# Conversion steps behind each slot's product, the states' last rows written in place, and x2 loads issued by GpSimd

## The chip, the cores and the metric

The kernel runs on one core of one Trainium2 chip. The metric is the device time of one execution in microseconds (us), as the median of three runs.

## What is computed

Attention between tokens and states in both directions, then two feed-forward layers over all 4608 rows (8 blocks of 512 token rows and 32 state rows):

```python
scores = scale * np.matmul(x, state.transpose(0, 1, 3, 2))   # x: (8, 8, 512, 64), state: (8, 8, 32, 64)
a = softmax(scores)                                          # with 1e-9 added to the sum
xread = np.matmul(a, state)
a2 = softmax(scale * np.matmul(state, x.transpose(0, 1, 3, 2)))
sread = np.matmul(a2, x)
x = concat([xread, sread]) -> (4352, 512)
h = ((x @ w1) * (x @ w2)) @ w3                               # w1, w2: 512 x 1024, w3: 1024 x 1024
x2 = h @ w_out                                               # 1024 x 512
h = x2 @ w_in                                                # 512 x 2048
out = (h * np.clip(h + 3.0, 0.0, 6.0) / 6.0) @ w_out2        # 2048 x 512
```

All inputs are float32.

## The kernel before

Matmuls take float32 operands split in a high part, rounded by ScalarE (`rnd`, L71), and the rest, made by VectorE (`rest`, L79); `mm3` (L87 to L90) multiplies the three products that matter. The order of the instructions on every engine is the order in which the program issues them.

The first part, up to about 480 us, goes over eight blocks `b` of the batch. The weights w3 and w_out are multiplied together ahead of it, and state and w1, w2 are folded into products p (`p_mm`, `p_split`), so that a block is eight **slots** `m`. A slot (`slot`, L646) does on TensorE two groups of six matmuls into the PSUM banks ps_ab, and ScalarE copies the first (asb, L522) while VectorE multiplies the second with it (ab, L524). Then `before()` runs, in which the next block's attention takes a step. Then x2_one multiplies an ab of two slots earlier with w3p; half-way through, `mid` splits this slot's ab (abh on ScalarE, abl on VectorE), and in slots of even number multiplies and splits the p that the slots from m + 2 on use (ph on ScalarE, pl on VectorE); attention takes another step there. Over a block attention's steps are scores in slot 0 (two banks ps_s), exponentials in slot 2, two transposes in slot 4 (ps_e) and the state read in slot 6 (ps_r); each is followed by the x2_one matmuls of the second half.

ps_ab, ps_p, ps_s, ps_e and ps_r take four PSUM banks in turn (`bank`, bufs=4). So the tile four allocations back must have been read out before a bank is written again.

Beside this runs the conversion of the second layer's weights (`stream2`, L426): 16 units, each in steps on VectorE (ts, hd, w, sl, cm), ScalarE (hd from raw, sh) and SP (the load raw, and writes of sh and sl to DRAM). A step counts 2 to 4 units of work, and ROOM says how many a slot may take; after `slot` returned, the loop took that many steps (L770 to L772):

```python
                slot(b, m, A, before, mid_)
                if b == 0:
                    step()
                room += ROOM[m]
                while room > 0:
                    room -= next(second, 99)
```

The load of the next x (`load_x`, L175: br and xr) is issued on SP in slot 6, in block 0 in slot 7.

In block 6 nothing is left to convert; w1 and w2 are split there for the states (`ws_split`, L570), five of eight, with five buffers. At the start of block 7 `s_block` (L577) passes all 256 state rows through the layer, eight steps of 24 matmuls of 256 columns (ps_sb). The state rows, sread's output, went to DRAM block by block (xs to xsd, L235) and come back in one load (xs_r, L744). The last three splits were made ahead of step 4, when their buffers were free.

The second part handles pairs `p` of blocks: `gates` (L927's matmuls, two levels of sums that save one of eight products), then `output` in 28 steps `v` of 12 matmuls (L1088). Step v splits the operand hlj of step v + 2 in a ring of three, high half on ScalarE and low half on VectorE, and `side(v)` takes steps of `combos(p + 1)`, which loads the next pair's x2 in two halves k (`x2_load`, L599: two DMAs each into the only buffer r), makes sums and splits them (xc). `per` tells how many combos steps a v takes. SP also issues all weight loads (`w_load`, L809), each of which waits until TensorE has let a buffer go. GpSimd issues the DMAs that add one g to another (`t_sum`, L895).

Of the kernel before, what the change touches and what calls it, by code (L numbers as in the profile page):

```python
# [7 lines left out]
F32 = mybir.dt.float32  # L8
F32R = mybir.dt.float32r
# [10 lines left out]
def attn_moe_kernel(tc, xt_d, xn_d, bd_d, wa, wb, wc, wi, wo, out):  # L20
# [48 lines left out]
    def rnd(out_, in_, eng):  # L69
        if eng == "A":  # L70
            nc.scalar.activation(out=out_, in_=in_, func=AF.Copy)  # L71
        elif eng == "P":
            nc.gpsimd.tensor_scalar(out=out_, in0=in_, scalar1=1.0, scalar2=0.0, op0=ALU.mult, op1=ALU.add)
        else:
            nc.vector.tensor_copy(out_, in_)
# [24 lines left out]
    w12 = {}  # L100
# [18 lines left out]

    ORDER = "oaoaoaoawwppppwwpppp"  # L120

    ROOM = (10, 7, 7, 6, 1, 6, 11, 9)


    class Pipe:
# [45 lines left out]


    x_t, A_t, st_t = {}, {}, {}

    def load_x(b):  # L175
        xr = att.tile([128, 4, 512], F32, tag="xr", name=f"xr{b}")
# [5 lines left out]
    def attention(b, fine=False):  # L182
# [47 lines left out]
            return ps  # L230

        def sread_out(ps):
            xs = att.tile([128, 4, NS], F32, tag="xs", name="xs")
            nc.scalar.copy(out=xs.rearrange("p c n -> p (c n)"), in_=ps[:, :4 * NS])
            nc.sync.dma_start(out=xsd[:, :, b * NS:(b + 1) * NS], in_=xs)  # L235
# [104 lines left out]
    with tc.manual_schedule():  # L340
# [226 lines left out]

        wsp = {}

        def ws_split(u):  # L570
            if u < 8:
                h, l = (wsq.tile([128, 1024], F32R, tag=f"ws{hl}", name=f"ws{hl}", bufs=5) for hl in "hl")
                rnd(h, w12[u // 4, u % 4], "A")
                rest(l, w12[u // 4, u % 4], h, "V")
                wsp[u // 4, u % 4] = h, l

        def s_block():  # L577
            for m in range(M1):
                if m == 4:
                    for u in range(5, 8):  # L580
                        ws_split(u)
                pss = []
                for i in range(2):
                    ps = bank(f"ps_sb{i}")
                    o = 512 * i + 128 * (m % 4)
                    for k in range(KD):
                        wh, wl = wsp[m // 4, k]
                        mm3(ps[:, :SR], wh[:, o:o + 128], wl[:, o:o + 128], xs_h[:, k, :], xs_l[:, k, :],
                            k == 0, k == KD - 1)
                    pss.append(ps)  # L590
                ab = ab_mul(pss[0], pss[1], SR)
                flush(1)
                h = ab_hi(ab, SR)
                queue.append((B, m, (h, ab_lo(ab, h, SR)), SR))
# [4 lines left out]
        def x2_load(p, k):  # L599
            r = x2r[p, k] = xb.tile([128, 2, 2, 512], F32, tag="r", name="r")  # L600
            for j in range(2):
                nc.sync.dma_start(out=r[:, :, j, :],
                                  in_=x2d[2 * p + j].rearrange("p (h k) f -> p h k f", k=2)[:, :, k, :])

        def combos(p):
# [122 lines left out]
        p_split(2)  # L728
        early_x2(3)
        second = stream2()  # L730
        room = 0
        for b in range(B):
            if 0 < b < B - 1:
                live.append(attention(b + 1))
            if b == B - 2:
                for _ in second:
                    pass
                close_pool("cvs")
                wsq = open_pool("wsq", bufs=1, side=right, reuse_waits="tile")
            if b == B - 1:  # L740
                xs_r = wsq.tile([128, KD, SR], F32, name="xs_r")
                xs_h = wsq.tile([128, KD, SR], F32R, name="xs_h")
                xs_l = wsq.tile([128, KD, SR], F32R, name="xs_l")
                nc.sync.dma_start(out=xs_r, in_=xsd)  # L744
                rnd(xs_h, xs_r, "A")
                rest(xs_l, xs_r, xs_h, "V")
                s_block()
                close_pool("wsq")
                close_pool("att")
                xb = open_pool("xb", bufs=1, side=right, reuse_waits="tile")  # L750
                first = combos(0)
            A = A_t.pop(b)
            for m in range(0 if b else 4, M1):
                if m == (6 if b else 7) and b + 2 < B:
                    load_x(b + 2)

                def before():
                    step()

                vn = 4 * b + m // 2 + 1  # L760

                def mid_():
                    if vn < 4 * B and m % 2 == 0:
                        p_mm(vn)
                        p_split(vn)
                    step()
                slot(b, m, A, before, mid_)
                if b == 0:
                    step()
                room += ROOM[m]  # L770
                while room > 0:
                    room -= next(second, 99)  # L772
                if b == B - 2 and m >= 3:
                    ws_split(m - 3)
                if b == B - 1:
                    for _ in range(1 if m == 0 else 4):
                        next(first, None)
            drain_att()
# [359 lines left out]
        for p in range(PAIRS):  # L1138
# [36 lines left out]
                def side(v):  # L1175
                    todo.get(v, nothing)()
            else:
                per = {1: 1, 22: 1, 23: 1, 25: 9}
                per.update({v: 2 for v in (7, 8, 9, 10, 11, 14, 15, 18, 19)})

                def side(v):
                    for _ in range(per.get(v, 0)):
# [62 lines left out]
```

## Time and profile before

| | |
|---|---|
| median of 3 runs | 1250.33 us (1249.41 to 1250.4) |
| the profiled execution | 1251.83 us, its span 1249.7 us |
| TensorE busy | 1197.9 us (96%), 6688 matmuls |
| VectorE busy | 863.1 us (69%) |
| ScalarE busy | 551.1 us (44%) |
| GpSimd busy | 36.1 us (3%) |
| mean granted TensorE clock | 0.988 |

The span goes from the first to the last instruction. A row of the timeline gives the start in us from the span's start, the duration, the engine, the line, what is written and read, and in brackets the idle time of the engine ahead of it with what ended it. Where the profile names an engine that had long been done, the wait was for another, often a DMA. The engines are PE (TensorE), PEld (its weight loads), DVE (VectorE), ACT (ScalarE), POOL (GpSimd) and SP.

### The profile page before, as it was taken

The page shows a single profiled execution, that of the slowest core. Times are in us where ns is not written, and L with a number is a line of the kernel's source. Part 1 is how long each engine was busy: PE and PEld are TensorE (multiplying, and loading weights), DVE is VectorE, ACT ScalarE, POOL GpSimd, SP SyncE. Part 2 cuts the span into 40 slices and gives each one's busy share as a digit, 9 for nine tenths or more (in the row PEclk, how much of TensorE's full clock was granted, in tenths as well). Part 3 has the DMA queues.
Part 4 walks back from the last instruction along what each step waited for, and adds up shares of the span by engine and source line. Part 5 has one row for each costly group of instructions (what it writes and reads, how often), then busy time and mean ns, then how long its engine had stood idle before and what let it go on. Part 6 is the DMA issues. An engine that isn't in the chain of part 4 may idle for free.

```text
span 1249.7 us, 17106 instructions
## 1 busy us (share of the span) xinstructions
PE 1197.9 (96%) x6688; PEld 943.3 (75%) x6688; DVE 863.1 (69%) x1220; ACT 551.1 (44%) x809; POOL 36.1 (3%) x47
## 2 busy tenths in 40 slices
PE   5989899999999999999999999999999999999997
PEld 2446677777777778877888788887888878888886
DVE  7976888887878463354768767687676876557483
ACT  3434454554545353244445434454344543334341
POOL 0000000000000000000001000010000100000100
PEclk9989999999999999999999999999999999999999
DMA  9751576585755201134889778997789977354973
GB/s 358 267 193 68 204 254 223 175 305 163 257 186 188 74 35 53 35 110 153 250 274 256 255 227 253 277 253 251 228 255 279 252 251 244 121 174 137 255 232 68
DMA packets 120256, 252.77 MB, mean 202 GB/s; under 512 B 45680, under 2 KB 63088, under 8 KB 113520
## 3 DMA queue, kind: packets, MB, share of 16 engines
q1 hardware_dynamic: 113696, 229.15, 53.3%
q0 software_dynamic: 5904, 21.50, 9.7%
q8 instruction: 52, 0.85, 0.3%
q10 hardware_dynamic: 576, 1.05, 0.2%
q14 instruction: 28, 0.23, 0.0%
HBM read 182.45 MB, written 47.71 MB: 184 GB/s over the span
## 4 chain that ended last, share of the span: by engine, by line
PE 75%; DVE 17%; ACT 3%; issue 2%; DMA 2%; ACTq 0%; DVEq 0%
PE ps L927 24%; PE ps_d L1088 17%; PE x L88 4%; PE x L89 4%; PE x L90 4%; PE ps_ab L88 4%; PE ps_ab L90 4%; PE ps_ab L89 4%; DVE hlj L79 2%; PE ps_w L414 2%; PE ps_hs L927 2%; PE ps_so L1101 2%; PE ps_p L360 2%; DMA r<-x2d 2%; DVE ab L524 1%
## 5 line engine op out<-in xcount | busy, mean ns | idle before, releaser
L927 PE MATMUL ps<-xc,wah 128*128 128x512 f32 x512 | 157.8, 389 | 0.0
L79 DVE TENSOR_TENSOR hlj<-g,hlj 128x1024 fp32r<-128x1024 f32 x84 | 102.2, 1216 | 31.1 <-ACT hlj L71 31.1
L1088 PE MATMUL ps_d<-hlj,wah 128*128 128x512 f32 x384 | 119.8, 391 | 1.4 <-DVE hlj L79 1.4
L857 ACT ACTIVATE rl<-c,half 128x512 f32<-128x512 f32 x96 | 69.5, 724 | 116.6 <-DVE c L827 67.8
L927 PE MATMUL ps<-xc,wbh 128*128 128x512 f32 x384 | 118.3, 389 | 0.0
L88 PE MATMUL x<-abh,w3ph 128*128 128x512 f32 (+1 forms) x288 | 114.4, 397 | 1.4 <-ACT x2s L83 1.1
L89 PE MATMUL x<-abl,w3ph 128*128 128x512 f32 (+1 forms) x288 | 110.4, 383 | 0.2 <-DVE half L824 0.2
L927 PEld LDWEIGHTS ps<-xc,wah 128*128 128x128 f32 x512 | 95.7, 188 | 19.5
L90 PE MATMUL x<-abh,w3pl 128*128 128x512 f32 (+1 forms) x288 | 109.9, 382 | 0.0
L71 ACT ACTIVATE hlj<-g 128x1024 fp32r<-128x1024 f32 x84 | 87.7, 1055 | 47.7 <-PE ps_d L1088 44.1
L88 PE MATMUL ps_ab<-Ah,ph 128*128 128x512 f32 x256 | 102.9, 402 | 1.6 <-DVE pl L79 0.9
L90 PE MATMUL ps_ab<-Ah,pl 128*128 128x512 f32 x256 | 100.6, 393 | 1.7 <-DVE pl L79 1.7
L89 PE MATMUL ps_ab<-Al,ph 128*128 128x512 f32 x256 | 100.6, 393 | 0.0
L927 PE MATMUL ps<-xc,wal 128*128 128x512 f32 x256 | 99.6, 389 | 0.0
L71 ACT ACTIVATE abh<-ab 128x512 fp32r<-128x512 f32 (+1 forms) x72 | 43.8, 608 | 125.3 <-DVE ab L524 125.3
L1088 PE MATMUL ps_d<-hlj,wbh 128*128 128x512 f32 x288 | 90.9, 393 | 4.9 <-DVE hlj L79 2.6
L1088 PEld LDWEIGHTS ps_d<-hlj,wah 128*128 128x128 f32 x384 | 72.1, 188 | 18.6 <-DVE hlj L79 3.7
L927 PEld LDWEIGHTS ps<-xc,wbh 128*128 128x128 f32 x384 | 72.0, 188 | 15.0
L524 DVE TENSOR_TENSOR ab<-ps_ab,asb 128x512 f32<-128x512 f32 x64 | 44.0, 687 | 50.8 <-PE ps_ab L90 45.6
L1088 PE MATMUL ps_d<-hlj,wal 128*128 128x512 f32 x192 | 74.7, 389 | 0.0
L927 PE MATMUL ps<-xc,wbl 128*128 128x512 f32 x192 | 74.7, 389 | 0.0
L79 DVE TENSOR_TENSOR abl<-ab,abh 128x512 fp32r<-128x512 f32 (+1 forms) x72 | 47.3, 658 | 39.3 <-ACT abh L71 39.3
(157 smaller groups left out, 2336.2 us busy)
## 6 DMA issues: line engine op xcount, KB each, us to landing
g<-g POOLq DMA_DIRECT2D x41, 512.0 KB, 7.1
wah<-swih SPq DMA_DIRECT2D x32, 512.0 KB, 4.4
wal<-swil SPq DMA_DIRECT2D x32, 512.0 KB, 5.5
wah<-swoh SPq DMA_DIRECT2D x32, 512.0 KB, 4.6
wal<-swol SPq DMA_DIRECT2D x32, 512.0 KB, 5.4
wbh<-swih SPq DMA_DIRECT2D x32, 384.0 KB, 4.9
wbl<-swil SPq DMA_DIRECT2D x32, 384.0 KB, 5.1
wbh<-swoh SPq DMA_DIRECT2D x32, 384.0 KB, 5.4
```

Of the source, the lines that this page charges most:

```text
L71: nc.scalar.activation(out=out_, in_=in_, func=AF.Copy)
L79: e.tensor_tensor(out=out_, in0=in_, in1=hi.bitcast(F32), op=ALU.subtract)
L88: nc.tensor.matmul(ps, lh, rh, start=first, stop=False)
L89: nc.tensor.matmul(ps, lh, rl, start=False, stop=False)
L90: nc.tensor.matmul(ps, ll, rh, start=False, stop=last)
L360: nc.tensor.matmul(ps[c][32 * q:32 * q + 32, 256 * i:256 * i + 256], st_t[b][r, 2 * c + j, 32 * k:32 * k + 32], w12[mm // 2, 2 * c + j][r, ...
L414: nc.tensor.matmul(w3_ps[m], t[:, o:o + 128], wout[k], start=k == 0, stop=k == M1 - 1)
L524: nc.vector.tensor_tensor(out=ab[:, :n], in0=psb[:, :n], in1=a[:, :n], op=ALU.mult)
L857: nc.scalar.activation(out=rl, in_=c, func=AF.Relu, bias=half, scale=sign / 6.0)
L927: nc.tensor.matmul(ps, u[:, k, :], v[:, k, :], start=first and k == 0 and i == 0, stop=k == 1 and i == 2, skip_group_check=True)
L1088: nc.tensor.matmul(d[name][q], a, x[:, k, :], start=i < 3 and n == 0 and z == 0, stop=n == NG - 1 and z == 2, skip_group_check=True)
L1101: nc.tensor.matmul(d["s"][q][:, 256 * e:256 * e + 256], a, x[:, n, :], start=i == 0 and n == 0 and z == 0, stop=i > 1 and n == NG - 1 and ...
```

## The change

1. ROOM's steps of `stream2` are taken inside `before()`, behind the ab product of the slot, instead of behind `slot`; two entries of ROOM differ by one.
2. The state rows of block 7 go from PSUM straight into xs_r; the other blocks' rows are loaded from DRAM in slot 2 of block 6. Six weight splits have buffers of their own and are made from slot 2 of block 6 on; the last two are made in steps 1 and 2 of `s_block`, in buffers that attention no longer uses. The split state rows xs_h and xs_l lie in attention's xn.
3. From pair 1 on, x2 loads are issued by GpSimd; the steps of `combos` are moved: none in v = 14, two each in v = 22 and 23.

```diff
-    ROOM = (10, 7, 7, 6, 1, 6, 11, 9)
+    ROOM = (10, 7, 6, 6, 2, 6, 11, 9)
...
         def sread_out(ps):
+            if b == B - 1:
+                nc.scalar.copy(out=xs_r[:, :, b * NS:], in_=ps[:, :4 * NS].rearrange("p (c n) -> p c n", c=4))
+                return
...
-        def ws_split(u):
-            if u < 8:
-                h, l = (wsq.tile([128, 1024], F32R, tag=f"ws{hl}", name=f"ws{hl}", bufs=5) for hl in "hl")
-                rnd(h, w12[u // 4, u % 4], "A")
-                rest(l, w12[u // 4, u % 4], h, "V")
-                wsp[u // 4, u % 4] = h, l
+        def ws_split(u, to):
+            h, l = to
+            rnd(h, w12[u // 4, u % 4], "A")
+            rest(l, w12[u // 4, u % 4], h, "V")
+            wsp[u // 4, u % 4] = h, l
 
         def s_block():
             for m in range(M1):
-                if m == 4:
-                    for u in range(5, 8):
-                        ws_split(u)
+                if m == 1:
+                    ws_split(6, [att.tile([128, 2, 512], F32R, tag=g, name="ws6").rearrange("p g f -> p (g f)")
+                                 for g in ("sN", "e2")])
+                if m == 2:
+                    t = att.tile([128, 4, 512], F32R, tag="xr", name="ws7").rearrange("p (g i) f -> p g (i f)", g=2)
+                    ws_split(7, [t[:, g] for g in range(2)])
...
             for j in range(2):
-                nc.sync.dma_start(out=r[:, :, j, :],
+                (nc.gpsimd if p else nc.sync).dma_start(out=r[:, :, j, :],
                                   in_=x2d[2 * p + j].rearrange("p (h k) f -> p h k f", k=2)[:, :, k, :])
...
             if b == B - 1:
-                xs_r = wsq.tile([128, KD, SR], F32, name="xs_r")
-                xs_h = wsq.tile([128, KD, SR], F32R, name="xs_h")
-                xs_l = wsq.tile([128, KD, SR], F32R, name="xs_l")
-                nc.sync.dma_start(out=xs_r, in_=xsd)
+                t = att.tile([128, T, DM], F32R, tag="xn", name="xs_hl").rearrange("p (i a) f -> p i (a f)", i=2)
+                xs_h, xs_l = (t[:, i].rearrange("p (k f) -> p k f", k=KD) for i in range(2))
...
                 def before():
+                    nonlocal room
                     step()
+                    room += ROOM[m]
+                    while room > 0:
+                        room -= next(second, 99)
...
-                room += ROOM[m]
-                while room > 0:
-                    room -= next(second, 99)
-                if b == B - 2 and m >= 3:
-                    ws_split(m - 3)
+                if b == B - 2 and m >= 2:
+                    if m == 2:
+                        xs_r = wsq.tile([128, KD, SR], F32, name="xs_r")
+                        n = (B - 1) * NS
+                        nc.sync.dma_start(out=xs_r[:, :, :n], in_=xsd[:, :, :n])
+                    ws_split(m - 2, [wsq.tile([128, 1024], F32R, tag=f"ws{hl}", name=f"ws{hl}", bufs=6) for hl in "hl"])
...
-                per = {1: 1, 22: 1, 23: 1, 25: 9}
-                per.update({v: 2 for v in (7, 8, 9, 10, 11, 14, 15, 18, 19)})
+                per = {1: 1, 25: 9}
+                per.update({v: 2 for v in (7, 8, 9, 10, 11, 15, 18, 19, 22, 23)})
```

What the order of the instructions makes of it, first on VectorE in slot 0 of block 2, from the slot's product ab on. Before:

```order
L524 TENSOR_TENSOR ab<-ps_ab_1605,asb 128x512
L79 TENSOR_TENSOR abl<-ab,abh 128x512
L79 TENSOR_TENSOR pl<-ps_p,ph 128x512 x2
L202 TENSOR_REDUCE mr<-ps_s 128x1
L203 TENSOR_SCALAR mr<-mr 128x1
L204 STREAM_TRANSPOSE sN<-ps_s 128x512
L202 TENSOR_REDUCE mr<-ps_s 128x1
L203 TENSOR_SCALAR mr<-mr 128x1
L204 STREAM_TRANSPOSE sN<-ps_s 128x512
L486 SCALAR_TENSOR_TENSOR w<-w,hd 128x512
L488 TENSOR_TENSOR w<-w,hd 128x512
L79 TENSOR_TENSOR sl<-w,sh 128x768
```

And with the change:

```order
L529 TENSOR_TENSOR ab<-ps_ab_1605,asb 128x512
L491 SCALAR_TENSOR_TENSOR w<-w,hd 128x512
L493 TENSOR_TENSOR w<-w,hd 128x512
L79 TENSOR_TENSOR sl<-w,sh 128x768
L79 TENSOR_TENSOR sl<-cm,sh 128x1024
L507 TENSOR_TENSOR cm<-w 128x256
L508 TENSOR_TENSOR cm<-w 128x256
L509 TENSOR_TENSOR cm<-cm,w 128x256
L510 TENSOR_TENSOR cm<-w,cm 128x256
L79 TENSOR_TENSOR abl<-ab,abh 128x512
L79 TENSOR_TENSOR pl<-ps_p,ph 128x512 x2
L204 TENSOR_REDUCE mr<-ps_s 128x1
```

The conversion steps (w, sl, cm) stood behind the slot's abl, pl and scores; now they stand ahead of them.

The second place is GpSimd's queue over the end of pair 0's gates and its output. Before, it held the sums alone:

```order
L895 DMA g_5157<-g_5158 128x1024
L895 DMA g_5158<-g_5160 128x1024
L895 DMA g_5157<-g_5158 128x1024
L895 DMA g_5158<-g_5160 128x1024
L895 DMA g_5157<-g_5158 128x1024
L895 DMA g_5158<-g_5160 128x1024 x2
L895 DMA g_5157<-g_5159 128x1024 x4
```

With the change:

```order
L904 DMA g_5153<-g_5154 128x1024
L904 DMA g_5154<-g_5156 128x1024
L609 DMA r<-x2d_79 128x2x512
L609 DMA r<-x2d_80 128x2x512
L904 DMA g_5153<-g_5154 128x1024
L904 DMA g_5154<-g_5156 128x1024
L904 DMA g_5153<-g_5154 128x1024
L904 DMA g_5154<-g_5156 128x1024 x2
L904 DMA g_5153<-g_5155 128x1024 x4
L609 DMA r<-x2d_79 128x2x512
L609 DMA r<-x2d_80 128x2x512
```

The first half's two loads moved from SP to behind the first two sums, the second half's to behind the last four.

The third place is ScalarE in the states' pass, steps 2 to 4 before:

```order
L71 ACTIVATE abh<-ab 128x256
L522 COPY asb<-ps_sb_4382 128x256
L71 ACTIVATE abh<-ab 128x256
L522 COPY asb<-ps_sb_4432 128x256
L71 ACTIVATE abh<-ab 128x256
L71 ACTIVATE wsh<-big_598 128x1024
```

And the start of the pass with the change:

```order
L71 ACTIVATE abh<-ab 128x512
L71 ACTIVATE wsh<-big_598 128x1024
L71 ACTIVATE xs_hl<-xs_r 128x1024
L527 COPY asb<-ps_sb_4279 128x256
L71 ACTIVATE abh<-ab 128x256
L71 ACTIVATE ws_4325<-big_643 128x1024
L527 COPY asb<-ps_sb_4329 128x256
```

The weight split of big_598 and its two followers moved from the middle of the pass to the end of block 6 and the first steps of the pass.

## Rows read from the trace of the kernel before

**Rows 1.** Waits of PE: engine, line, releaser: us in total, times, longest.

```profile
PE ps_e L213 <- DVE ab L524: 8.6, 4, 2.7
PE ps_s L198 <- ACT ph L71: 4.2, 1, 4.2
PE ps_d L1088 <- DVE hlj L79: 4.0, 8, 0.8
...
PE ps_d L1088 <- ACT hlj L71: 2.1, 3, 0.8
PE ps_sb L90 <- DVE wsl L79: 1.8, 3, 0.8
...
PE x L88 <- ACT x2s L83: 1.1, 2, 0.9
```

**Rows 2.** Busy time by stretches; behind POOL the granted clock, DMA share, GB/s.

```profile
148.00:158.00 10.00, 9.80 (x36) 6.46 (x37) 7.79 (x14) 5.50 (x11) 0.00 (x0) 0.83 0.86 337
...
506.00:516.00 10.00, 8.97 (x62) 8.56 (x62) 3.21 (x5) 1.47 (x5) 0.00 (x0) 0.83 0.00 0
...
360.00:420.00 60.00, 60.00 (x514) 46.09 (x513) 45.67 (x72) 30.01 (x50) 0.00 (x0) 1.00 0.43 149
```

**Rows 3.** Groups of DVE from 120 to 400 us, and timelines in block 2's slot 4.

```profile
L79 DVE TENSOR_TENSOR abl<-ab,abh 128x512 fp32r<-128x512 f32 x39 | 26.8, 686 | 19.6 <-ACT abh L71 19.6
L79 DVE TENSOR_TENSOR pl<-ps_p,ph 128x512 fp32r<-128x512 f32 x40 | 25.7, 684 | 3.9 <-ACT ph L71 3.9
...
234.52 0.69 DVE L524 TENSOR_TENSOR ab<-ps_ab,asb 128x512 f32<-128x512 f32 x1
...
235.26 0.66 PE L213 MATMUL ps_e<-ident,e 128*128 128x128 f32 x4 [2.01 <-DVE ab L524]
```

**Rows 4.** Timelines around the load of xr for block 2, and its landing.

```profile
131.16 0.68 DVE L524 TENSOR_TENSOR ab<-ps_ab,asb 128x512 f32<-128x512 f32 x1
...
137.74 1.22 DVE L473 SCALAR_TENSOR_TENSOR w<-raw,ts 128x1024 f32<-128x1024 uint32 x1
...
139.88 0.42 SPq L179 DMA_DIRECT2D xr<-in_xt_dram  x1
...
DMA to landing us min/median/max: 8.2/8.2/8.2
...
148.20 1.08 PE L198 MATMUL ps_s<-xr,br 128*64 128x512 f32 x4 [4.23 <-ACT ph L71]
```

**Rows 5.** Timelines of PE and DVE in slot 0 of block 2.

```profile
202.43 0.39 PE L88 MATMUL x<-abh,w3ph 128*128 128x512 f32 x1
...
208.49 0.39 PE L88 MATMUL ps_ab<-Ah,ph 128*128 128x512 f32 x1
...
211.10 0.65 DVE L486 SCALAR_TENSOR_TENSOR w<-w,hd 128x512 f32<-128x512 f32 x1
...
215.52 0.43 DVE L505 TENSOR_TENSOR cm<-w,cm 128x256 f32<-128x256 f32 x1
```

**Rows 6.** Timeline of ACT ahead of block 2.

```profile
202.81 0.85 ACT L71 ACTIVATE sh<-w 128x768 fp32r<-128x768 f32 x1 [4.19 <-DMA swoh<-sh]
```

**Rows 7.** Timelines of DVE and PE in the states' pass.

```profile
504.44 3.50 DVE L79 TENSOR_TENSOR wsl<-big,wsh 128x1024 fp32r<-128x1024 f32 x3 [0.52 <-ACT wsh L71]
...
482.38 0.39 PE L89 MATMUL ps_sb<-xs_l,wsh 128*128 128x256 f32 x1 [1.07 <-DVE xs_l L79]
```

**Rows 8.** Timelines in pair 0's output; last, landing of the sums g, 660 to 700 us.

```profile
681.87 0.86 POOL L895 DMA_DIRECT2D g<-g  x1 [2.62 <-DVE hlj L79]
...
687.55 0.69 DVE L79 TENSOR_TENSOR xc<-r,xc 128x512 fp32r<-128x512 f32 x1 [0.70 <-ACT xc L71]
...
691.74 1.18 SPq L602 DMA_DIRECT2D r<-x2d  x2
...
698.19 0.63 ACT L71 ACTIVATE xc<-r 128x512 fp32r<-128x512 f32 x1 [5.99 <-DMA r<-x2d]
...
DMA to landing us min/median/max: 6.2/7.9/9.8
```

More of the change, by code (lines that the diff above doesn't have):

```diff
@@ L173, in attn_moe_kernel @@
     x_t, A_t, st_t = {}, {}, {}
+    xs_r = None
+    room = 0
     def load_x(b):
@@ L730, in attn_moe_kernel @@
         second = stream2()
-        room = 0
         for b in range(B):
```

## The prediction

> **What bounds the kernel now.** I read the busy table first: TensorE is busy for 1197.9 of 1249.7 us, so the change can only win what TensorE stands still, and what it then runs at half clock. The waits of TensorE [rows 1] say what it stood still for. After the start-up, whose code is the same in both kernels, three places are left. In the slots of blocks 0 to 4 (120 to 360 us) the rows on ps_e and ps_s, the x row, and two smaller ones of 0.9 and 0.3 us give 8.6 + 4.2 + 1.1 + 0.9 + 0.3 = 15.1 us. In the pass over the states (480 to 510 us) the wsl row has 1.8 us. In the outputs of pairs 0 to 2 the two ps_d rows have 4.0 + 2.1 = 6.1 us, about 2 for each pair.
>
> The table by stretches adds the clock [rows 2]. Five stretches of 10 us were granted 0.83, which is full speed but for one piece at 1.2 in place of 2.4 GHz (the first and the last of the five are shown). Each lost (1 - 0.83) x 10 = 1.7 us. Three of them follow gaps in the slots of 4.23, 2.72 and 2.44 us; two lie in the states' pass. Between 360 and 420 us, where block 4's second half and block 5 run, TensorE is busy throughout.
>
> Why does TensorE wait in the slots? In block 2 the second transpose of slot 4 waits 2.01 us for VectorE's product ab [rows 3]: that product reads the PSUM bank that the transpose is to fill. VectorE is late because it loses time elsewhere: for abl it waits for ScalarE's abh, 19.6 us in 39 slots, and for pl another 3.9 [rows 3]. The other kind of gap, 4.23 us in block 1, is put down to ScalarE's ph, but the load of xr is issued at 139.88 and lands 8.2 us later, at 148.1, just when TensorE goes on at 148.20 [rows 4]. SP came to it so late since a load ahead of it waited for the conversion step of 137.74.
>
> **The change, part by part.** The sum is made against the profiled execution, 1251.83 us (span 1249.7); the median of the runs, 1250.33, is 1.5 lower.
>
> *Conversion steps behind the product.* Nothing is removed: the same steps stand between two ab products, in another order. Now they stand ahead of abl and pl, so the 19.6 + 3.9 us in which VectorE waited for ScalarE have work in them, 4.7 us in each of five blocks. That is more than any of the slot-4 gaps. In block 1 the load's gap shrinks too: the step that held SP started at 137.74, 6.6 us after its slot's product at 131.16 [rows 4]; now only four cm and two shifts of 0.42 us stand between the two, 2.5 us behind a product of 0.7, while abl, pl and Al follow. So xr is issued about 3.3 us earlier, and 4.23 becomes 0.9.
>
> What is late next is pl. In slots 0 and 6 the attention takes two (one) of the four rotating banks, and the next slot's first product must go into the banks of this slot's p, which pl still reads. Slot 0 of block 2 shows the room: from the end of the ab matmuls (202.43) to the next slot's (208.49) are 6.1 us [rows 5]. After the change VectorE does in that time the product (starts 0.3 later, 0.7), the conversion steps, abl (0.7) and the first pl (0.65): 2.35 us and the steps. The steps that now stand there ran from 211.10 to 215.95 in the trace [rows 5]: 4.85 us. So TensorE waits 2.35 + 4.85 - 6.1 = 1.1 us. By the durations of the same instructions the other four blocks carry 3.5 to 3.9 us there, and wait 0 to 0.2: together 1.5. From slot 6 only the second matmul group is held, 1.4 us later, so that the steps and Al may take 5.1 us; they take 4.3 to 5.8, which gives 1.3 over four blocks. That is the floor: 2.8 us, if VectorE comes to these slots without arrears.
>
> Above it lies ScalarE. The step sh now stands ahead of abh and ph, and sh once waited 4.19 us for its own earlier DMA to leave the buffer [rows 6]. In the order of the change two sh lie close together at the entries of blocks 1 and 3 (sh in slot 6 or 7 and again in slot 0). I bound this by nothing and 4.2 us at each of the two and take half, 4.2 in all. Block 1's slot 4 keeps its 1.4, since ScalarE's exponentials and sh come ahead of its ph in slot 2; block 1's first product waits some 0.8 for Al, which stood ahead of the steps of block 0's slot 6 and now stands behind them; the rest of the load's gap is 0.9; the x row keeps 0.9; and one gap may be long enough for one more piece at half clock, 1.7. After the change: 2.8 + 4.2 + 1.4 + 0.8 + 0.9 + 0.9 + 1.7 = 12.7, against 15.1 + 3 x 1.7 = 20.2. **Gain 7.5 us**, between 0 and 17.4 (20.2 less the floor). The two edits to the table of units (7 to 6, 1 to 2) are in the steps counted; each is one unit of about 0.4 us, covered by the bubbles above.
>
> *States.* The last three weight splits take ScalarE and VectorE 3.5 us in one row, at 504.44, and TensorE waits for them [rows 7]: 1.8 + 0.2 us, and a piece at half clock, 1.7. Now one more is made in block 6, where VectorE has nothing to convert, and two in the first three steps of the pass, where VectorE has two short instructions a step to do. **Gain 3.7 us**, 2.0 if the clock falls all the same. That the last rows go straight to their tile gains nothing: the gap at 482.38 [rows 7] is ScalarE's and VectorE's, who make wsh, then xs_h and xs_l one behind the other; the order there is the same afterwards.
>
> *x2 loads from GpSimd.* The buffer r is free when its last reader ends, at 688.24 (687.55 + 0.69), but SP is held by the weight loads ahead of it and issues at 691.74; ScalarE then waits 5.99 us for the landing, and the split of the ring behind it makes TensorE late [rows 8]. GpSimd has issued its last sum at 681.87 and is free, so the first load goes out at about 688.3. Loads by SP took 6.4 us, GpSimd's own sums 6.2 to 9.8 [rows 8]; I take 7.5, near the middle, since the last sum is still under way then. It lands at 695.8. The step that wants it also moves one step of 2.7 us on, so ScalarE comes to it at about 694.9 and waits 1 us, where the ring has 3 us in hand (two steps of 2.7 less 2.4 for its two halves). The moved steps give VectorE 0.7 us more in each of steps 22 and 23, behind two output steps of 3.3 us that are longer than TensorE's 2.7; I leave 0.5 us a pair for that. **Gain 6.1 - 1.5 = 4.6 us**, from -1 (landing 9.8 us after, and the arrears in full) to 6.1. The loads' waits now stand on GpSimd's queue: behind them come the next pair's sums, which are issued four steps of the gates later. On SP nothing but weight loads moves up.
>
> Here a rule stands against the change. What the row shows is that the issue, not the transfer, was late, by 3.5 us. The Trainium skill ("DMA: Bandwidth & Descriptors", Issuing engines are not separate DMA queues) says that all queues end on the same 16 DMA engines and that another issuing engine saves only the time to initiate. By it the two issues [rows 8], 1.2 us a pair, are the most that could be won: 3.5 in place of 4.6. No run here shows yet which holds; the row speaks for the wait of SP's queue being won as well.
>
> Sum: 7.5 + 3.7 + 4.6 = 15.8; 1251.8 - 15.8 = 1236.0, and 1.5 lower as the median: **1234.5 us**.
>
> **Rivals.**
> 1. *The gaps move and keep their size.* Every wait on ab becomes one on pl. For it: the room of 6.1 us against 7.2 in block 2. Against: the other blocks' smaller steps. States and loads alone: 1250.3 - 8.3 = 1242.0. Chance 0.20.
> 2. *Nearly all clears*: only the floor of 2.8 stays, and the loads win 6.1: 1250.3 - (17.4 + 3.7 + 6.1) = 1223.1. For it: between 360 and 420 us TensorE did not wait at all. Against: sh. Chance 0.15.
> 3. *Slower: pl behind sh.* If sh waits for its DMA in slot 0 of all five blocks, each loses 1.1 + 4.2 and a piece at half clock, 1.7: 35 us against the 20.2 that go: 1250.3 + 14.8 - 8.3 = 1256.8. It decides from 5.7 us a block on (28.5 in five). Against: one such wait of any length in the trace before [rows 6]. Chance 0.07.
> 4. *The loads land no earlier*, because the transfer shares its engines with the sums and weights (the 9.8 us of rows 8): 4.6 less: 1239.1. Chance 0.08. The rule of the Trainium skill named above would end between this and the forecast.
>
> **The numbers.** The forecast has 0.50. The range takes in rivals 1, 2 and 4: 1223 to 1246, the upper end being rival 1 with the states' clock and the loads at their poor ends. A change under 0.2% (2.5 us) could not be told from none. Faster: all but rival 3 and the far end of 1, 0.90; same 0.04; slower 0.06.
>
> **What would show it.** Right: no TensorE wait on ab at ps_e in blocks 2 to 4; new, short waits on pl or ph at the first ab matmul of slots 1 and 7, under 2 us; no wait on wsl, while those on xs_h and xs_l stay; r issued by GpSimd at once when the buffer is free, and ps_d waits of under 2 us in all. Wrong: waits at ps_ab of 3 us and more with sh ahead of ph on ScalarE, several pieces at half clock there, or ScalarE still standing for r.

## The result and the profile after

The changed kernel takes 1231.79 us (median of 4 runs, 1230.34 to 1234.02), the kernel before 1250.0 in the same series: a ratio of 0.9856, 95% interval 0.9837 to 0.9875. That is 2.7 us under the forecast of 1234.5 and inside the range. The profiled execution took 1234.02 us with a span of 1232.2, so the spans differ by 17.5 us. Where these lie is another matter, and there the forecast was wrong twice, in opposite directions.

I cut both traces into stages, from the first matmul of one to the first of the next. Here "slots" goes from block 1's state product (ps_r, the second of eight, in slot 6 of block 0) to block 7's (in slot 6 of block 6); start-up and most of block 0 lie ahead of it.

| stage, us | before | after | gain | forecast |
|---|---|---|---|---|
| slots | 346.68 | 343.81 | 2.9 | 7.5 |
| from block 7's state product to the states' pass | 9.79 | 9.79 | 0 | 0 |
| the pass over the states | 43.13 | 38.82 | 4.3 | 3.7 |
| slots of block 7 | 52.59 | 51.45 | 1.1 | not named |
| gates of pair 0 | 76.16 | 77.13 | -1.0 | not named |
| outputs of pairs 0, 1, 2 | 79.61, 79.82, 79.70 | 76.16 each | 10.7 | 4.6 |
| other gates, last output, start and end | | | -0.5 | 0 |

The waits of TensorE after, the view of [rows 1] (the first letters name the matmul that waited):

```profile
PE ps_ab L88 <- DVE pl L79: 10.0, 6, 3.9
...
PE ps_e L215 <- DVE ab L529: 1.6, 2, 1.3
PE ps_sb L89 <- DVE xs_hl L79: 1.1, 1, 1.1
PE ps_sb L88 <- ACT xs_hl L71: 0.7, 1, 0.7
...
PE ps L936 <- DMA wal<-swil: 0.6, 1, 0.6
PE ps_ab L89 <- DVE Al L79: 0.5, 1, 0.5
```

Of [rows 1] the rows on ps_s, wsl and ps_d are gone, and ps_e fell from 8.6 to 1.6 us. The new row on pl is the largest: three waits of 3.95, 2.34 and 2.42 us, each at the first ab matmul of slot 1, in blocks 1, 2 and 3. Behind each the clock falls, as it does at the start of the states' pass. Stretches after, the view of [rows 2] (length, busy time of PE, PEld, DVE, ACT, POOL, granted clock, DMA share, GB/s):

```profile
148.00:158.00 10.00, 6.05 (x20) 4.54 (x19) 6.67 (x13) 5.79 (x12) 0.00 (x0) 0.83 0.83 301
206.00:216.00 10.00, 7.66 (x27) 5.39 (x24) 8.48 (x17) 3.02 (x8) 0.00 (x0) 0.83 0.72 268
264.00:274.00 10.00, 7.58 (x27) 5.74 (x26) 6.88 (x12) 6.53 (x12) 0.00 (x0) 0.83 1.01 356
476.00:486.00 10.00, 8.24 (x40) 7.11 (x39) 3.91 (x5) 3.78 (x6) 0.00 (x0) 0.83 0.01 2
```

What stands ahead of the second of these waits is to be read on three engines: timelines after of ACT, DVE and PE, from block 1's slot 7 to block 2's slot 1.

```profile
200.87 0.85 ACT L71 ACTIVATE sh<-w 128x768 fp32r<-128x768 f32 x1 [4.61 <-DMA swoh<-sh]
201.62 1.04 ACT L71 ACTIVATE sh<-cm 128x1024 fp32r<-128x1024 f32 x1
202.56 0.62 ACT L71 ACTIVATE abh<-ab 128x512 fp32r<-128x512 f32 x1
...
203.22 0.69 DVE L79 TENSOR_TENSOR abl<-ab,abh 128x512 fp32r<-128x512 f32 x1 [2.08 <-ACT abh L71]
...
209.82 1.28 DVE L79 TENSOR_TENSOR pl<-ps_p,ph 128x512 fp32r<-128x512 f32 x2
...
210.56 0.65 PE L88 MATMUL ps_ab<-Ah,ph 128*128 128x512 f32 x1 [2.34 <-DVE pl L79]
```

ScalarE stands 4.61 us until the transfer of the last sh is done, with abh behind it; VectorE has done its steps and waits 2.08 us for that abh; slot 0's own steps then start late, pl later still, and TensorE waits. There are four such waits of sh after, of 5.44, 4.61, 2.52 and 4.36 us (waits of ACT; before, the first of these rows had 4.7 us and the second 0.2):

```profile
ACT sh L71 <- DMA swoh<-sh: 9.0, 2, 4.6
ACT sh L71 <- DMA swih<-sh: 8.0, 2, 5.4
```

In pair 0's output the loads went as forecast. The step that wants r waits 1.19 us in place of 5.99 [rows 8], and no ps_d wait is left (timelines after of POOL and ACT):

```profile
681.34 1.47 POOL L609 DMA_DIRECT2D r<-x2d  x2 [5.82 <-DVE xc L79]
...
688.85 0.63 ACT L71 ACTIVATE xc<-r 128x512 fp32r<-128x512 f32 x1 [1.19 <-DMA r<-x2d]
```

### The profile page after: what moved, and what is told of

Same layout as the page of the kernel before. It is cut to its first block, busy times and chain, and to the rows that moved or that the text cites. A ratio compares the mean times of both kernels' runs of the same rounds, so it can differ in the third digit from the quotient of the medians.

```text
span 1232.2 us, 17120 instructions
## 1 busy us (share of the span) xinstructions
PE 1191.2 (97%) x6688; PEld 943.4 (77%) x6688; DVE 862.7 (70%) x1220; ACT 551.9 (45%) x809; POOL 44.7 (4%) x59
## 4 chain that ended last, share of the span: by engine, by line
PE 82%; DVE 10%; DMA 4%; ACT 2%; issue 1%; SPq 0%; ACTq 0%; DVEq 0%
PE ps_d L1097 25%; PE ps L936 24%; PE x L88 4%; PE ps_ab L88 4%; PE ps_ab L90 4%; PE x L89 4%; PE x L90 4%; PE ps_ab L89 4%; PE ps_w L419 2%; PE ps_hs L936 2%; PE ps_so L1110 2%; PE ps_p L365 2%; DMA swoh<-sh 1%; DVE sl L79 1%; DMA wal<-swil 1%
## 5 line engine op out<-in xcount | busy, mean ns | idle before, releaser
L88 PE MATMUL ps_ab<-Ah,ph 128*128 128x512 f32 x256 | 105.2, 411 | 10.8 <-DVE pl L79 10.0
L904 POOL DMA_DIRECT2D g<-g x41 | 35.7, 871 | 1102.9 <-DVE c L836 593.9
```

Of the source, the lines that this page charges most:

```text
L88: nc.tensor.matmul(ps, lh, rh, start=first, stop=False)
L904: nc.gpsimd.dma_start(out=to, in_=of, accum_op=ALU.add)
```

## The experiments

**One part at a time.** Four kernels start from the kernel before and take one part of the change each. Their diffs are pieces of the change's own:

```diff
 # steps_alone: the room loop inside before(), ROOM as changed; nothing else
+                    room += ROOM[m]
+                    while room > 0:
+                        room -= next(second, 99)
 # states_alone: ws_split with its tiles given, six splits in block 6, last rows in place
+                if b == B - 2 and m >= 2:
 # gpsimd_alone
+                (nc.gpsimd if p else nc.sync).dma_start(out=r[:, :, j, :],
 # per_alone: the loads stay on SP
+                per = {1: 1, 25: 9}
+                per.update({v: 2 for v in (7, 8, 9, 10, 11, 15, 18, 19, 22, 23)})
```

> Only the conversion steps' new place (with the two changed entries of ROOM); states and x2 loads as before. If the parts add, block 7's state read comes 2.7 us earlier than before (471.1 to 468.4 us) and nothing after it changes: 1247.3 us. My prediction had 7.5 us for this part, 1242.5. If the parts help each other, less than 1 us, 1249 or more.

> Only the states' part: splits buffered, last rows in place. If the parts add: from the state read of block 7 to the first gates 4.3 + 1.1 = 5.4 us less than before (105.5 us), 1244.6 us; the waits on xs_h and xs_l at the start of the pass stay at 0.7 and 1.1 us. My prediction had 3.7 us, 1246.3. If the direct write of the last rows saved something, those two waits would be gone.

> x2 loads from GpSimd, combos steps at the places of before. If the late issue was the cause, the load goes out 3.2 us earlier, lands 2.1 us earlier by the trace of the changed kernel, and each output takes 76.2 to 76.7 us in place of 79.6: 1240 us. If the moved steps were needed too, ScalarE stands 3 to 4 us for r in step 14 and an output takes 78 us or more: 1245 us.

> Combos steps moved, x2 loads still on SP. If the late issue was the cause, the load still lands 45.4 us into the output, ScalarE reaches it one step (2.7 us) later than before, at 42 us, and stands 3.3 us: an output takes 78 us or more, 1245 us. If the place of the step alone decides, the ring has enough in hand and an output takes 76.2 us: 1239.5 us.

The kernel before took 1251.23 us in this series.

| kernel | median, us | ratio (95%) | slots | pass | outputs 0, 1, 2 |
|---|---|---|---|---|---|
| steps_alone | 1246.17 | 0.9958 (0.9944 to 0.9973) | 343.02 | 42.95 | 79.89, 79.65, 80.06 |
| states_alone | 1247.38 | 0.9967 (0.9957 to 0.9978) | 348.71 | 37.31 | 80.10, 79.73, 79.57 |
| gpsimd_alone | 1244.30 | 0.9948 (0.9929 to 0.9967) | 347.88 | 43.07 | 77.62, 78.55, 76.39 |
| per_alone | 1258.72 | 1.0061 (1.0038 to 1.0084) | 351.59 | 41.38 | 82.17, 83.28, 82.37 |

Each part does its work in its own stage: the steps 3.7 us in the slots, the states 5.8 in the pass (which has no piece at half clock there; two before, one after the change). The gains of the first three add up to 15.8 us by the medians, that of the fourth is -7.5, and the change won 18. So the moved combos steps are worth something only with the loads off SP. On SP they lose: SP comes to the second half's load only behind one more round of weight loads (timeline of SP, then waits of PE, in per_alone):

```profile
697.04 0.32 SPq L809 DMA_DIRECT2D wah<-swoh  x1
697.46 0.38 SPq L809 DMA_DIRECT2D wal<-swol  x1
697.93 1.18 SPq L602 DMA_DIRECT2D r<-x2d  x2
```

```profile
PE ps_d L1088 <- ACT hlj L71: 9.1, 3, 3.3
```

The issue comes 44.4 us into the output in place of 38.9 (691.74 in [rows 8]), and each output is 2.6 to 3.5 us longer than before. With GpSimd's loads the same move takes another 4.1 us off the three outputs (77.62 + 78.55 + 76.39 - 3 x 76.16). GpSimd alone leaves 1.8 us of ps_d waits:

```profile
PE ps_d L1088 <- DVE hlj L79: 1.8, 5, 0.5
PE ps L927 <- DMA wal<-swil: 1.2, 1, 1.2
```

The second row is new, lies in pair 0's gates and is taken up below.

The slots column has to be read with the clock. A piece at half clock costs 1.7 us, and where the slots' code is the same the number of pieces in them still differs: 3 before, 4 in gpsimd_alone, 4 in states_alone, 6 in per_alone. Less 1.7 us a piece, which is an estimate, these four come to 341.1 to 341.9 us, and the five kernels with the new place and the changed table (the changed kernel, steps_alone, k0_by_sp, loads_scalar and split5_later, with 2 or 3 pieces) to 337.9 to 338.9. So the place is worth some 3 us apart from the clock, and 5.1 us with it by the medians of steps_alone and of the kernel before.

**Is it sh's wait for its transfer that makes the pl waits?** To take that wait away without a race, the high halves are sent from another tile that is never written again; all else stays.

```diff
                         x = t.bitcast(F32)[:, 256 * of:256 * (of + n)].rearrange("p (s e) -> p s e", e=256)
+                        if hl == 0:
+                            x = w12[0, 0][:, None, :256].to_broadcast([128, n, 256])
```

> The changed kernel, but the seven pieces of the high half of each converted unit go to memory from a finished weight tile in place of sh, same bytes, same shapes, same place in SP's queue: so ScalarE's next write of sh no longer waits for a transfer. What it leaves out: the high halves of the second layer's weights are not the right numbers. Theory (with the steps ahead of mid, ScalarE's sh stands ahead of abh and ph and waits there for the transfer of the last sh, and that is what makes the three pl waits at block entry, 3.95, 2.34 and 2.42 us, and the half-clock pieces behind them, 1.7 us each): the four waits of sh for a transfer (5.4, 4.6, 2.5, 4.4 us) go, VectorE pl waits of PE fall from 10.0 us to at most 3, the slots from the first to the seventh state product shorten from 343.8 to 332 to 336 us, the time is 1220 to 1225 us. Rival (VectorE has too much in these slots, sh only shows it): the pl waits stay at 8 us or more in all, time 1229 us or more.

Measured: 1226.99 us (ratio 0.9816, 0.9801 to 0.983), slots 338.33. It lies between the two: ScalarE has no wait for a transfer left, and two of the three pl waits shrink to 1.01 and 0.95 us and lose their half-clock pieces, but the first stays (timelines of PE and DVE):

```profile
140.91 0.39 PE L88 MATMUL x<-abh,w3ph 128*128 128x512 f32 x1
...
150.29 0.55 PE L88 MATMUL ps_ab<-Ah,ph 128*128 128x512 f32 x1 [3.36 <-DVE pl L79]
207.23 0.51 PE L88 MATMUL ps_ab<-Ah,ph 128*128 128x512 f32 x1 [1.01 <-DVE pl L79]
...
142.90 0.68 DVE L531 TENSOR_TENSOR ab<-ps_ab,asb 128x512 f32<-128x512 f32 x1
...
148.08 0.96 DVE L79 TENSOR_TENSOR sl<-w,sh 128x768 fp32r<-128x768 f32 x1 [1.30 <-DMA swil<-sl]
```

In block 1 VectorE itself stands 1.30 us for the transfer of the low half sl, with abl and pl behind it. It also comes to that slot late: its product ab starts at 142.90 us, 2.0 us after TensorE has gone on from the ab matmuls (140.91), where in block 2 it is 0.3. In block 2 what is left is VectorE's own work ahead of pl, and its 1.01 us is the 1.1 that the prediction worked out for that slot. So sh's wait makes part of the pl waits, and the work that a slot holds makes the rest.

**Does an even spread help?** This kernel changes the table alone.

```diff
-    ROOM = (10, 7, 6, 6, 2, 6, 11, 9)
+    ROOM = (8, 7, 7, 7, 4, 7, 9, 8)
```

> The changed kernel with the conversion steps spread more evenly over a block's slots, ROOM (8, 7, 7, 7, 4, 7, 9, 8) for (10, 7, 6, 6, 2, 6, 11, 9), same sum. Theory (two units' sh fall within 13 us where slots 6, 7 and 0 carry 30 of 51 units of room, so the second waits for the transfer of the first): the waits of sh for a transfer fall from 16.9 us to under 8, the pl waits from 10.0 to about 5, time 1224 to 1229 us. Rival (slot 4, which ROOM spared, has no room on VectorE): new waits of 3 us or more open at slots 4 and 5, time 1231 to 1237 us.

Measured: 1230.27 us (0.9839, 0.9824 to 0.9854), slots 339.02. The pl waits at blocks 2 and 3 are gone, that of block 1 is 2.92 us, and the rival's waits came too: 1.54, 0.64, 0.28 and 2.48 us on ps_e in slot 4. Both were partly right, and the gain on the changed kernel is within the measurement.

**The start of the states' pass.**

```diff
-                    ws_split(m - 2, [...])
+                    if m < 7:
+                        ws_split(m - 2, [...])
...
                 rest(xs_l, xs_r, xs_h, "V")
+                ws_split(5, [...])
```

> The changed kernel with the sixth weight split of the states' pass (ws_split(5)) moved from the last slot of block 6 to behind xs_h and xs_l. Theory (the waits of 0.69 and 1.07 us at the start of the states' pass are the order on ScalarE and VectorE, with that split ahead of xs_h and xs_l, and not the way of the last rows): both waits shrink to under 0.5 us together, the half-clock piece at 480 us goes or stays with them, the stretch from the seventh state product to the pass shortens from 9.79 to 8.0 to 9.0 us, time lower by 1 to 3.5 us, 1228 to 1231 us. Rival (the last rows themselves come late): the waits stay at 1.7 us, time 1231 to 1232.5 us.

Measured: 1230.8 us (0.9845, 0.9831 to 0.986). The stretch ahead of the pass shortens from 9.79 to 8.94 us; the wait of 0.69 us is gone, that on the low half is 0.87 for 1.07. So the order on ScalarE was the first wait's cause; the 0.87 is the pair xs_h, xs_l itself. More is left than the 0.5 expected, but the rival is out: the rows were there.

**Who issues the loads?** Two kernels: the first half (k = 0) by SP again, and all the next pairs' loads by ScalarE.

```diff
-                (nc.gpsimd if p else nc.sync).dma_start(out=r[:, :, j, :],
+                (nc.gpsimd if p and k else nc.sync).dma_start(out=r[:, :, j, :],    # k0_by_sp
+                (nc.scalar if p else nc.sync).dma_start(out=r[:, :, j, :],          # loads_scalar
```

> The changed kernel with the first half (k = 0) of each next pair's loads issued by SP again, the second half (k = 1) by GpSimd. Theory (the wait of 0.64 us for wal in pair 0's gates comes from the first half's loads being issued by GpSimd 605 us in, beside the weight loads; the gain in the outputs is all the second half's): the first gates stage goes from 77.13 to 76.16 us, the outputs stay at 76.16 us each, time lower by 1.0 us, 1230.8 us. Rival (the first half's loads too were held up in SP's queue): outputs of 77 us or more, time 1233 us or more.

Measured: 1230.77 us (0.9849, 0.9833 to 0.9866), pair 0's gates 76.16 us, the outputs 76.16 each: as the theory had it; the medians differ by 1.0 us, which their intervals do not separate. In every profiled execution with k = 0 on GpSimd pair 0's gates take 77.13 to 77.79 us, in every one with it on SP or ScalarE 76.16.

> The changed kernel with the next pairs' loads issued by ScalarE in place of GpSimd. Theory (what the loads gained is that they no longer stand behind the weight loads and stores in SP's row of instructions; any other row would do): the outputs of pairs 0 to 2 stay within 76.2 to 76.8 us each, time 1231 to 1234 us. First rival (ScalarE's own row takes it back: a load that waits there for r or for room holds up the roundings behind it): outputs of 77.5 us or more, time 1236 us or more. Second rival (the gain is GpSimd's own way of moving data and not the row it stands in): outputs of 79 us or more as before the change, time 1241 us or more.

Measured: 1234.03 us (0.9876, 0.986 to 0.9892); outputs 76.99, 77.51, 77.33. It ends between theory and first rival, and the second rival is out. Timeline of ACT in pair 0's output:

```profile
683.56 1.19 ACTq L609 DMA_DIRECT2D r<-x2d  x2
687.65 0.63 ACT L71 ACTIVATE xc<-r 128x512 fp32r<-128x512 f32 x1 [3.04 <-DMA r<-x2d]
688.19 1.99 ACT L71 ACTIVATE hlj<-g 128x1024 fp32r<-128x1024 f32 x2
```

ScalarE's own row takes part of it back: the issue comes 41.0 us into the output, where GpSimd's came at 35.7 and SP's, before, at 38.9, and ScalarE stands 3.04 us for the data, with two splits of hlj run late behind it. The load lands 45.1 us into the output, as before (45.4; GpSimd's at 43.2). So against the kernel before the gain of these outputs is most likely the moved steps', which can move once the load does not stand on SP: in per_alone it landed at 50.2. No run has ScalarE's loads with the steps at their old places, so this is not shown.

**Less work in each slot.** After the change block 5 has no conversion from its slot 2 on (VectorE's last step starts at 385.7 us). So the units of a block are cut from 57 to 50, which spreads the same steps to the end of block 5; with it go the two edits above that helped (split5_later, k0_by_sp).

```diff
-    ROOM = (10, 7, 6, 6, 2, 6, 11, 9)
+    ROOM = (6, 7, 7, 7, 2, 7, 7, 7)      # best_light
+    ROOM = (8, 7, 7, 8, 2, 8, 9, 8)      # best_even
```

> The changed kernel with k = 0 loads by SP (k = 1 by GpSimd), the sixth weight split behind xs_h and xs_l, and lighter steps that reach to the end of block 5: ROOM (6, 7, 7, 7, 2, 7, 7, 7), 50 in place of 57. Theory (a slot's load of conversion work, and two transfers of sh or sl within 13 us, set the pl waits; block 5 has room that nothing uses): the wait of 3.9 us near 152 us falls under 1.5, those near 210 and 268 us under 0.5, the slots from the first to the seventh state product take 334 to 338 us against 343.8, the pass starts 0.85 us earlier, gates 76.16 us; time 1220 to 1225 us. Rival (the work only moves: what blocks 4 and 5 now carry waits there): slots 340 us or more, time 1228 to 1231 us.

> As the kernel with lighter steps, but with ROOM (8, 7, 7, 8, 2, 8, 9, 8), the same 57 of the changed kernel, slot 4 kept light. Theory (the even spread took the waits near 210 and 268 us, its slot 4 of 4 opened the ps_e waits of 1.54, 0.64 and 2.48 us): slots 337 to 340 us, ps_e waits under 2 us in all, time 1225 to 1229 us. Rival (slot 4's waits come from the two slots ahead of it): ps_e waits of 4 us or more, slots 340 us or more, time 1229 us or more.

Measured: best_light 1215.69 us (0.9727, 0.9713 to 0.974), best_even 1228.46 (0.9829, 0.9816 to 0.9842). best_light wins 16.1 us on the changed kernel and is the best version here: slots 328.60 us in place of 343.81, no piece at half clock between start-up and the end. So 15.2 us of it are the light table's, 5.1 of them for three half-clock pieces. The even one at the full 57 has a time within its theory's range but failed it in the stage: slots 340.71, with 7.0 us of waits on ps_e. The three spreads of the 57 that were run gave 339.02 to 343.81 us, so in these tables the amount decides more than the spread; other spreads of 57 were not tried. ScalarE still waits 6.8 us for transfers of sh (17.0 after), but the slots have the room for it. What TensorE still waits for there (waits of PE; the row of 2.1 is in the start-up):

```profile
PE ps_ab L90 <- DVE pl L79: 2.1, 1, 2.1
PE ps_ab L88 <- DVE pl L79: 1.5, 3, 0.9
...
PE ps_e L215 <- DVE ab L529: 0.5, 2, 0.3
```

**Is the place of the steps then worth anything?** The last kernel is best_light with the steps back behind the whole slot.

```diff
                 def before():
                     step()
-                    room += ROOM[m]
-                    while room > 0:
-                        room -= next(second, 99)
...
                 slot(b, m, A, before, mid_)
+                room += ROOM[m]
+                while room > 0:
+                    room -= next(second, 99)
```

> The kernel with the lighter steps (ROOM (6, 7, 7, 7, 2, 7, 7, 7), k = 0 loads by SP, the sixth weight split behind xs_h and xs_l), but with the conversion steps back behind the whole slot, where they stood before the change. Theory (the share of work in a slot decides, and the place ahead of mid only sets where sh and sl wait: with light slots the place is worth little): slots from the first to the seventh state product 329 to 333 us against 328.6, time 1215 to 1220 us. Rival (the place is what the change gained there, 2.7 us or more of its own, as 346.7 to 343.8 and 343.0 us showed at the full load): slots 334 us or more with waits for pl behind sl, time 1221 us or more.

Measured: 1228.34 us (0.9824, 0.981 to 0.9837), slots 343.08. The rival holds, and by more than it asked, though the waits are on ps_e and ps_s and not on pl: with light slots the place is worth 14.5 us in the slots and 12.7 by the medians, at the full load it was worth 2.9 and 5.1. Of the 14.5, three half-clock pieces, which best_light does not have, make 5.1. The group of abl on DVE from 120 to 400 us tells why (busy, mean of one, then the idle time ahead of it): of after, of best_light, of light_old_place, and of sh_own_source.

```profile
L79 DVE TENSOR_TENSOR abl<-ab,abh 128x512 fp32r<-128x512 f32 x40 | 27.4, 686 | 10.8 <-ACT abh L71 10.8
```

```profile
L79 DVE TENSOR_TENSOR abl<-ab,abh 128x512 fp32r<-128x512 f32 x42 | 28.8, 685 | 2.7 <-ACT abh L71 2.5
```

```profile
L79 DVE TENSOR_TENSOR abl<-ab,abh 128x512 fp32r<-128x512 f32 x40 | 27.4, 686 | 19.7 <-ACT abh L71 19.7
```

```profile
L79 DVE TENSOR_TENSOR abl<-ab,abh 128x512 fp32r<-128x512 f32 x40 | 27.4, 686 | 7.8 <-ACT abh L71 7.8
```

Before, VectorE lost 19.6 us there [rows 3]; in the old place it loses as much with the light table. In the new place the steps fill this time, but at the full load 10.8 us of it come back. Only 3.0 of these go with sh's waits for transfers (sh_own_source, without such a wait, still has 7.8); the rest comes with the load itself, as the 2.7 of best_light shows. The old place keeps its other price too: xr is issued at 138.67 in place of 136.05 us, and TensorE waits 4.19 us for it, and 5.8 us on ps_e:

```profile
PE ps_e L215 <- DVE ab L529: 5.8, 5, 1.8
PE ps_s L200 <- DMA xr<-in_xt_dram: 4.2, 1, 4.2
```

## Why the prediction was right, and where it was wrong

The total was right because two terms were off by nearly the same amount in opposite directions: 4.6 us too much for the steps, 5.1 too little for the loads. Nothing ties the two errors to each other, so that part is luck.

**Conversion steps: 7.5 forecast, 2.9 measured (5.1 by the medians of steps_alone).** What it said of the mechanism held: the waits on ab at ps_e went from 8.6 to 1.6 us, xr was issued 3.6 us earlier (136.27 for 139.88) and its gap went, and pl was late next. The step that failed is the sum "2.8 + 4.2 + 1.4 + 0.8 + 0.9 + 0.9 + 1.7 = 12.7"; it came to some 17.2. Two of its terms were too small. The floor of 2.8 (VectorE's work ahead of pl) is 5.8 by sh_own_source (3.36 + 1.01 + 0.95 + 0.27 + 0.20), since block 1, put at 0 to 0.2, holds a rest(sl) that waits 1.30 us for its own transfer, and VectorE comes to its slot 0 2.0 us behind TensorE (0.3 was taken), held by the steps of the slot ahead: the condition "without arrears" did not hold there. The 1.3 expected from slot 6 did not come. The half-clock term, "one more piece", was three: 5.1 in place of 1.7. The 4.2 for sh was near as waiting time, 3.4 (the differences between after and sh_own_source at the three entries: 0.59, 1.33, 1.47), but in three blocks where two were named, and two of the three half-clock pieces are gone in sh_own_source. The rest came out lower: Al 0.46, xr and x nothing, ps_e 1.6 (block 1's 0.32 for the 1.4, and 1.27 in block 4, where none was expected), and 0.88 on a pl at 121.65 us, which the prediction counted before (its 0.9) and left out after. Rival 1 was the nearer picture of this stage: the gaps moved and kept most of their size, and the sign given for "wrong" (3 us at ps_ab, sh ahead of ph, several half-clock pieces) is what the trace shows.

**Loads: 4.6 forecast, 10.7 less 1.0 measured.** Each step of the chain came as written: the issue 3.2 us earlier in the output (35.7 us from its start for 38.9), a landing after 7.5 us, a wait of 1.2 us on ScalarE where 1 was said. The step that failed is its price, the 6.1 us from the waits of TensorE; and the 0.5 us a pair left for VectorE's arrears was not needed, since no ps_d wait is left. Output 0 is 79.61 us long before and 76.16 after, with the same 336 matmuls, so 3.45 us were to be had in it, where the waits show 2.0. The reason is in the timeline of PE before, in output 0:

```profile
698.82 0.39 PE L1088 MATMUL ps_d<-hlj,wbl 128*128 128x512 f32 x1
699.82 0.50 PE L1088 MATMUL ps_d<-hlj,wbh 128*128 128x512 f32 x1 [0.61 <-ACT hlj L71]
701.08 0.51 PE L1088 MATMUL ps_d<-hlj,wbh 128*128 128x512 f32 x1 [0.76 <-DVE hlj L79]
701.42 0.39 PE L1088 MATMUL ps_d<-hlj,wbl 128*128 128x512 f32 x1
```

In a run without waits these matmuls start 0.227 us apart (76.16 / 336). Here the starts are 1.00 and 1.26 us apart, an excess of 0.77 and 1.03 where the brackets say 0.61 and 0.76, and the next one starts 0.34 us later in place of 0.23. The bracket counts from the modelled end of the matmul ahead, which lasts 0.39 us but blocks its successor for 0.23 only: it leaves out about 0.16 us of each wait, and 0.11 behind it. Together that is 0.27 us a wait, a third and more of its bracket (0.18 to 0.76 us in this output). The four waits make 3.1 of the 3.45 us in this way. The busy times of the two outputs show it once more (same columns as the stretches above; before, then after):

```profile
652.81:732.42 79.61, 77.58 (x337) 62.68 (x336) 61.38 (x72) 36.94 (x45) 4.30 (x5) 1.00 0.85 256
```

```profile
645.60:721.76 76.16, 76.16 (x338) 63.08 (x336) 61.72 (x72) 37.40 (x45) 5.77 (x7) 1.00 0.90 265
```

The idle time before is 79.61 - 77.58 = 2.03 us, the cost 3.45. The cost of the loads themselves on GpSimd, 1.0 us in pair 0's gates, was not foreseen: "behind them come the next pair's sums" looked at GpSimd's queue, while the first half's loads, at 605 us, make a weight load late: they go out 36 us into that stage, just ahead of a round of SP's weight loads, where SP's own went out at 31, and the wal issued at 605.56 lands after 10.4 us, where k0_by_sp's of the same round took 9.0.

```profile
615.96 0.50 PE L936 MATMUL ps<-xc,wal 128*128 128x512 f32 x1 [0.64 <-DMA wal<-swil]
```

**The rule weighed against it.** The two issues take 1.18 us on SP [rows 8] and 1.47 on GpSimd, so the issue itself got no shorter. Still gpsimd_alone, which changes the issuing engine and nothing else, took 6.6 us off the three outputs, 2.2 a pair on average, less 1.5 in pair 0's gates. What was won is the place in line: on SP the load waits behind weight loads that wait for buffers of their own. The Trainium skill ("DMA: Bandwidth & Descriptors", Issuing engines are not separate DMA queues) says that initiating on several engines saves only the sequencer's time to initiate. By it 1.2 us a pair was the most, and the outputs of gpsimd_alone decide against it. Its other half, that all transfers share the same engines, agrees with the weight load that TensorE waits for at 615.96.

**States: 3.7 forecast, 4.3 in the pass.** The wsl waits went and one of two half-clock pieces with them, as said. That the direct way of the last rows gains nothing held as far as the pass goes: the waits at its start are 0.69 and 1.07 us in both kernels (of [rows 7] the second), and split5_later shows that the first is the order on ScalarE. The 1.1 us in block 7 was not named: before, its last slot waits 0.31 and 0.23 us for abh and its low half at 573 us, which by the step lengths cost 1.1; after, it does not.

## What to carry to other kernels

Filling an engine's idle time with work from a side stream pays only as far as that work does not itself wait and the time holds it; here the place of the steps was worth 3 to 5 us with a full table and 13 to 14 us with one an eighth lighter, so move the work and thin it together, out to the end of the room that there is. Price a wait of a pipelined engine by the length of its stage against one without waits, not by the sum of the idle brackets. A load that stands behind others in an engine's row is moved by the row it stands in: test the pieces together, since the moved steps lost 7.5 us alone and won 4.1 us with the loads on another row.

## What was not expected of the hardware

The clock does not follow the length of a gap as the prediction took it to. The states' pass begins with the same two waits, 0.69 and 1.07 us, in the changed kernel and in k0_by_sp; the first was granted 0.83 from 476 to 486 us (shown above), the second full clock, and its pass takes 37.31 us in place of 38.82. In split5_later a wait of 3.31 us at 151 us is followed by full clock, where 3.95 us at the same place after the change, 3.12 us there in k0_by_sp, and 2.34 and 2.42 us at the next two after the change, were each followed by a piece at 1.2 GHz. The same stretches, first of k0_by_sp, then of split5_later:

```profile
476.00:486.00 10.00, 8.47 (x57) 7.78 (x58) 3.94 (x5) 2.52 (x5) 0.00 (x0) 1.00 0.01 2
```

```profile
148.00:158.00 10.00, 6.81 (x30) 5.67 (x31) 7.63 (x13) 6.16 (x13) 0.00 (x0) 1.00 0.71 275
```

So 1.7 us for such a piece can come or go between two kernels that wait alike, and a difference of that size in one profiled execution is no evidence of an edit. What decides it was not settled here.
